# Retention attention and two expert layers in one kernel: attention reordered chunk by chunk over the batches

## The chip, the cores and the metric

The kernel runs on one core of a Trainium2 chip. The metric is the device time of one execution in microseconds (us). Three runs of the kernel before took 872.59, 873.83 and 874.82 us; the median is 873.83 us. Profiles are of a single execution, whose own time stands in the table below.

## The reference

Three stages follow one another. The first is a linear attention with a decaying state (4 batches, 8 heads, 768 tokens, 64 elements a head), the second a layer of 512 to 2048 to 512 with a piecewise quadratic activation, the third one of 512 to 1024 to 512 with a softmax gate and a normalisation. The weights are float64.

```python
for t in range(S):                       # attention, per batch and head
    state = gamma * state + outer(k[t], v[t])
    y[t] = scale * (q[t] @ state)
x = y.transpose(0, 2, 1, 3).reshape(3072, 512)
h = x @ w_in                             # first layer
g = where(h >= 1, h, where(h <= -1, 0, (h + 1) ** 2 / 4))
x = g @ w_out
h = x @ w_in2                            # second layer
solu = h * softmax(h)
out = (layernorm(solu) * g_ln) @ w_out2
```

## The kernel before

**Attention in chunks.** A unit u is one chunk of 128 tokens of one batch with all 8 heads (4 pairs of heads); there are 24. With `b, c = divmod(u, NCH)` (NCH = 6) the units run through a batch before the next begins. For each unit `att_scores` (L532) multiplies keys and queries on TensorE into PSUM `pa`; VectorE multiplies the scores by a decay table with the causal mask (`sm`, L557) and, for a chunk that isn't the first of its batch, the queries by another table (`qn`, L539). `att_products` adds the product with the state (`cross`) and the product of masked scores and values (`within`, L602 and L607), and forms the chunk's own contribution to the state (`state`, L616) from the keys, which were decayed before by GpSimd for the units 0 to 3 (L544) and by ScalarE for the others (L548). ScalarE decays the one state tile (L694) and VectorE adds the contribution (L704 for a first chunk, L706 else). In the units 0 to 11 the state tile holds two heads in the diagonal blocks of a 128x128 matrix and `cross` is four products of the full array (mode "words", L591); from unit 12 (`QUAD`) on it holds 64x64 blocks and `cross` is eight products of 64 rows by 64 columns (mode "quarters", L587). For that the second half of the head pairs is kept with swapped partitions: `load_swapped` fetches the queries and keys of the units 12 to 23 in three transfers each, and `swap_tables` exchanges the tables in between.

**Blocks.** Four units fill one block of 512 tokens, `x`. Blocks 0 and 1 are split into a high and a low part (L646, L650) and go through the first layer with plain products: `moe_h` (L748) and `moe_out` (L805), twelve products of 512 columns each per hidden block f. In the order `segs`, block 0 takes f = 0 to 5, block 1 f = 0 to 11, then each the rest. Blocks 2 to 5 go in two pairs through a version with seven products in place of eight (L986, L1137). The second layer follows (L1460, L1571, L1603). The units 0 to 3 run before the first `moe_h`, the units 4 to 15 between the hidden blocks of the first two blocks, the units 16 to 23 between the products of the first pair.

**Weights.** `conv` turns a float64 weight block into a high and a low float32 part: a load of 512 KB (L380), three ops on ScalarE, five on VectorE (L398, L401 of 256 columns' length; L404, L407, L426 of 512). The blocks f = 0 to 5 of both matrices are the first twelve.

**The order of the work.** All tasks go to a planner (`Plan`). It takes a cost for each, works back from TensorE's sequence to a goal for every other task (`late`), and lists the tasks engine by engine, the earliest goal first among those that can start (`listed`). The order that it finds is written out for TensorE, VectorE, ScalarE, GpSimd and SP; each engine then works in that order and waits for its operands. SP issues all transfers, with at most eight under way. The value `due` in most calls isn't used for goals. TensorE's tasks may swap places within a window of six during the first part.

**The start.** The prologue issues 40 warm-up products (L1212). `tables` (L453) loads the decay table in four transfers of 128 KB (L458), multiplies it on VectorE (L460) and masks it on GpSimd (L461); the table for the queries is a transfer of 256 KB (L465) and a product on GpSimd (L466).

## Time and profile before

| | |
|---|---|
| median of three runs | 873.83 us |
| profiled execution | 875.24 us |
| its span, first to last instruction | 873.2 us |
| mean granted TensorE clock | 0.991 of full speed |
| TensorE (PE) busy | 847.3 us, 97% |
| VectorE (DVE) busy | 716.4 us, 82% |
| ScalarE (ACT) busy | 577.6 us, 66% |
| GpSimd (POOL) busy | 164.1 us, 19% |
| moved by DMA | 176.09 MB, mean 202 GB/s |

TensorE's busy time counts the modelled ends of pipelined products, so consecutive products overlap in it; the step from the start of one group to the start of the next is the better measure of what a group occupies. The share of 97% is a mean over stages. The idle time that a row gives stands ahead of its group, with the work whose end released it; "issue" means that the profile shows no such work.

### The profile page before, as it was taken

The page shows a single profiled execution, that of the slowest core. Times are in us where ns is not written, and L with a number is a line of the kernel's source. Part 1 is how long each engine was busy: PE and PEld are TensorE (multiplying, and loading weights), DVE is VectorE, ACT ScalarE, POOL GpSimd, SP SyncE. Part 2 cuts the span into 40 slices and gives each one's busy share as a digit, 9 for nine tenths or more (in the row PEclk, how much of TensorE's full clock was granted, in tenths as well). Part 3 has the DMA queues.
Part 4 walks back from the last instruction along what each step waited for, and adds up shares of the span by engine and source line. Part 5 has one row for each costly group of instructions (what it writes and reads, how often), then busy time and mean ns, then how long its engine had stood idle before and what let it go on. Part 6 is the DMA issues. An engine that isn't in the chain of part 4 may idle for free.

```text
span 873.2 us, 13826 instructions
## 1 busy us (share of the span) xinstructions
PE 847.3 (97%) x4752; PEld 690.7 (79%) x4752; DVE 716.4 (82%) x1326; ACT 577.6 (66%) x1145; POOL 164.1 (19%) x421
## 2 busy tenths in 40 slices
PE   7799999999999999999999999999999999999997
PEld 6678878777777778778878877887888888888886
DVE  3999989989956887999999768899977777777761
ACT  2888857689767998885448666444655555555552
POOL 3000000000000101100141110011374444444443
PEclk7999999999999999999999999999999999999999
DMA  8956797999779999778665555767020102020001
GB/s 318 391 196 231 254 311 269 319 332 321 241 229 345 383 290 377 252 301 283 225 220 196 192 184 189 245 240 241 8 78 19 66 25 73 26 73 24 26 25 48
DMA packets 70261, 176.09 MB, mean 202 GB/s; under 512 B 7984, under 2 KB 18608, under 8 KB 70192
## 3 DMA queue, kind: packets, MB, share of 16 engines
q1 hardware_dynamic: 70192, 175.22, 57.5%
q8 instruction: 37, 0.61, 0.3%
q14 instruction: 32, 0.26, 0.1%
HBM read 124.86 MB, written 50.33 MB: 201 GB/s over the span
## 4 chain that ended last, share of the span: by engine, by line
PE 68%; DVE 15%; ACT 9%; DMA 4%; issue 3%; SPq 1%; POOL 0%; ACTq 0%; DVEq 0%
PE op L1603 15%; PE hp L986 15%; PE h2p L1460 12%; PE yp L1137 11%; PE acc L805 4%; PE hp L748 4%; DVE go L1104 3%; PE tp L1571 2%; PE pa L532 2%; DVE g L907 2%; DMA w_raw<-in_w_out_dram 1%; DVE sm L557 1%; ACT cs L727 1%; PE pa L607 1%; DVE ws L872 1%
## 5 line engine op out<-in xcount | busy, mean ns | idle before, releaser
L1137 PE MATMUL yp<-go,left 128*128 128x512 f32 x672 | 153.9, 390 | 0.9 <-ACT cs L1160 0.7
L1137 PEld LDWEIGHTS yp<-go,left 128*128 128x128 f32 x672 | 126.0, 188 | 28.2 <-ACT cs L1160 1.6
L986 PE MATMUL hp<-xoh,left 128*128 128x512 f32 x448 | 122.4, 395 | 2.0 <-issue 1.1
L1100 ACT ACTIVATE go<-g 128x512 fp32r<-128x512 f32 x112 | 69.4, 628 | 51.6 <-PE yp L1137 28.2
L986 PEld LDWEIGHTS hp<-xoh,left 128*128 128x128 f32 x448 | 82.6, 188 | 21.4 <-issue 1.9
L1603 PE MATMUL op<-w,lh 128*128 128x512 f32 x384 | 93.2, 390 | 0.9 <-ACT lh L1578 0.9
L1460 PE MATMUL h2p<-w,x2h 128*128 128x512 f32 x336 | 92.5, 397 | 0.5 <-ACT h2p L1473 0.4
L1603 PEld LDWEIGHTS op<-w,lh 128*128 128x128 f32 x384 | 71.9, 188 | 16.3 <-ACT lh L1578 1.5
L1104 DVE TENSOR_TENSOR go<-g,go 128x512 fp32r<-128x512 f32 x112 | 77.9, 704 | 7.1 <-ACT go L1100 6.3
L805 PE MATMUL acc<-gh,w 128*128 128x512 f32 x256 | 72.5, 401 | 1.5 <-ACT acc L790 1.5
L1460 PEld LDWEIGHTS h2p<-w,x2h 128*128 128x128 f32 x336 | 61.3, 188 | 13.1 <-ACT h2p L1473 1.1
L748 PE MATMUL hp<-xh,w 128*128 128x512 f32 x256 | 69.9, 399 | 1.7 <-DVE cs L730 1.0
L986 PE MATMUL hp<-xol,left 128*128 128x512 f32 x224 | 69.1, 390 | 0.0
L1036 POOL TENSOR_TENSOR g<-gl,gh 128x512 f32<-128x512 f32 x16 | 22.5, 1404 | 243.4 <-ACT gh L1010 92.8
L1522 DVE TENSOR_REDUCE st<-h2p 128x1 f32<-128x512 f32 x24 | 16.5, 686 | 56.7 <-PE h2p L1460 56.7
L729 ACT ACTIVATE cs<-cs 128x512 f32<-128x512 f32 x96 | 59.3, 625 | 1.2
L748 PEld LDWEIGHTS hp<-xh,w 128*128 128x128 f32 x256 | 47.0, 189 | 12.9 <-DVE cs L730 1.9
L805 PEld LDWEIGHTS acc<-gh,w 128*128 128x128 f32 x256 | 46.2, 188 | 13.7 <-ACT acc L790 2.3
L1460 PE MATMUL h2p<-w,x2l 128*128 128x512 f32 x168 | 51.9, 390 | 0.0
L1578 ACT ACTIVATE lh<-tp 128x512 fp32r<-128x512 f32 x48 | 28.4, 596 | 33.3 <-PE tp L1571 20.4
L986 PEld LDWEIGHTS hp<-xol,left 128*128 128x128 f32 x224 | 42.1, 188 | 9.1
L1530 ACT ACTIVATE e<-h2p,st 128x512 f32<-128x512 f32 x24 | 16.5, 689 | 48.0 <-DVE st L1525 48.0
(130 smaller groups left out, 1757.0 us busy)
## 6 DMA issues: line engine op xcount, KB each, us to landing
left<-left SPq DMA_DIRECT2D x112, 512.0 KB, 4.6
left<-wsh SPq DMA_DIRECT2D x64, 256.0 KB, 4.7
kv<-in_kv_t_dram SPq DMA_DIRECT2D x24, 512.0 KB, 7.0
w_raw<-in_w_in_dram SPq DMA_DIRECT2D x24, 512.0 KB, 7.6
w_raw<-in_w_out_dram SPq DMA_DIRECT2D x24, 512.0 KB, 7.5
left<-w SPq DMA_DIRECT2D x48, 256.0 KB, 3.1
qk<-in_qk_t_dram SPq DMA_DIRECT2D x12, 512.0 KB, 6.4
x2r<-x2d SPq DMA_DIRECT2D x12, 512.0 KB, 5.3
```

Of the source, the lines that this page charges most:

```text
L532: pe.matmul(e["qp"][o][:, p, :], e["qk"][r, 1, p, :], e["qk"][r, 0, p, :], start=True, stop=True)
L729: q = ACT(A512, lambda: sc.activation(c["t"], c["t"], AF.Square), (r,), due + 0.5)
L748: pe.matmul(c["h"], cut(w, part, k), r[:, k, :], start=(n == 0), stop=(n == 3 * KD - 1))
L805: pe.matmul(acc[d], cut(w, l, d), r, start=(first and fresh and n == 0), stop=(last and n == 2), skip_group_check=True)
L986: pe.matmul(e[bank], w[i][:, k * 128:(k + 1) * 128], x[j][:, k], start=(first and m == 0), stop=(last and m == 3 * KH - 1), skip_group_che ...
L1036: h = POOL(1.1, lambda: gp.tensor_tensor(out=g(1, 1), in0=cell["s3"], in1=cell["s5"], op=ALU.add), (x, e["s5"][1], e["c11"]), v + 4)
L1100: sc.activation(t[:, 0], quarters_g(n)[q], AF.Copy)
L1104: ve.tensor_tensor(out=lo, in0=quarters_g(n)[q], in1=fl(hi), op=ALU.subtract)
L1137: pe.matmul(e["banks"][j], w[:, s, j * 128:(j + 1) * 128], g[t], start=(n == 0 and c == 0), stop=(n == NP - 1 and c == 2))
L1460: pe.matmul(bank[b], x[t][:, AT[key], k], w2i[key, k]["w"][:, part], start=(start and m == 0), stop=(stop and m == 3 * KH - 1), skip_group ...
L1578: sc.activation(c["h"][:, 4 * n:4 * n + 4], c["tp"][:, n].rearrange("a (j c) -> a j c", j=4), AF.Copy)
L1603: pe.matmul(o["p"], c[l][:, f_], w2o[f_]["w"][:, part], start=(k == 0 and f_ == 0), stop=(k == 2 and f_ == NF2 - 1))
```

## The change

The units are numbered chunk first: `c, b = divmod(u, CPB)`, so each block holds one chunk of all four batches, and the first block holds the first chunks, which have no state to read. Each batch has its own state tile of 64x64 blocks. All cross products are quarters; the swapped loads, the swapped tables and the cleared state are gone. The head order inside `x` is changed to match what the quarters write, and the rows of `w_in` are put into that order by loading each block in two transfers of 64 partitions. Rows of the output are written where the token order needs them. In the first block the values are loaded ahead of the keys in separate halves, and the state products of its four units, with a ScalarE copy into the state tiles, are issued behind the first two hidden blocks' `moe_h`. The decay table is read as one row of 4 KB and spread over the partitions by two products with a column of ones. The scores of unit 3 use other PSUM banks, and `xh` of unit 3 is made in halves. The scores of unit 1 come before the products of unit 0. In the planner, a TensorE task that follows another TensorE task is ready when the engine is free, not a fixed tail later. Some small constants of the second layer move into a pool opened after attention. Bookkeeping of the accumulator banks (`acc["banks"]`) is left out here, as is unchanged context.

```diff
             for u in after.get(t, ()):
                 todo[u] -= 1
-                u.base = max(u.base, t.start if t is u.gate or t in u.forced else t.end)
+                u.base = max(u.base, t.start if t is u.gate or t in u.forced else free["PE"] if t.eng == u.eng == "PE" else t.end)
...
-    st = attp.tile([128, NPAIR, 128], F32, tag="state", name="state", bufs=1)
+    states = [attp.tile([128, NPAIR, D], F32, tag=f"state{b}", name="state", bufs=1) for b in range(B)]
...
-    def load_swapped(dst, src):
-        n = NPAIR // 2
-        ax = (slice(None),) * (len(dst.shape) - 3)
-        nc.sync.dma_start(dst[(slice(None), *ax, slice(0, n))], src[(slice(None), *ax, slice(0, n))])
-        for h in range(2):
-            nc.sync.dma_start(dst[(slice(64 * h, 64 * h + 64), *ax, slice(n, 2 * n))],
-                              src[(slice(64 - 64 * h, 128 - 64 * h), *ax, slice(n, 2 * n))])
...
-            nc.sync.dma_start(raw.rearrange("p a t -> p (a t)"), src.bitcast(U32))
+            if heads:
+                d, s_ = raw.rearrange("p (r c) t -> p r (c t)", r=2), src.bitcast(U32).rearrange("(r i) c -> i r c", r=2)
+                for g in range(2):
+                    nc.sync.dma_start(d[64 * g:64 * g + 64], s_[:, :, 512 * g:512 * g + 512])
+            else:
+                nc.sync.dma_start(raw.rearrange("p a t -> p (a t)"), src.bitcast(U32))
...
+        l = DMA(512, load, (), due - 9, (raw_s,), run=2 if heads else 4, ahead=ahead or CAHEAD, issues=2 if heads else 1)
...
+        row = DMA(4, lambda: nc.sync.dma_start(rows, xtab_d[0:128:64].rearrange("(a r) p c -> a r (p c)", a=1)), (), -56.0)
         for o in range(2):
-            ds = [DMA(128, partial(lambda o, d: nc.sync.dma_start(dmat[64 * d:64 * d + 64, o], xtab_d[64 * o:64 * o + 64]), o, d), (), -56.0)
-                  for d in range(2)]
-            m = DVE(U512, partial(lambda o: ve.tensor_tensor(out=dmat[:, o], in0=dmat[:, o], in1=vdec[:, o::2].to_broadcast([128, NPAIR, C]), op=ALU.mult), o), ds + [a], -56.0)
+            def spread(o):
+                c[o] = ps_h.tile([128, 512], F32, tag="h", name="spread")
+                pe.matmul(c[o], ones, rows[:, o], start=True, stop=True)
+
+            def mult(o):
+                ve.tensor_tensor(out=dmat[:, o], in0=c[o].rearrange("a (p c) -> a p c", p=NPAIR), in1=vdec[:, o::2].to_broadcast([128, NPAIR, C]), op=ALU.mult)
+            s_ = Slot("h")
+            w = plan.pe(0.9, partial(spread, o), (row,), (s_,), mode="words")
+            m = DVE(U512, partial(mult, o), [w, a])
+            s_.used(m)
...
-    def swap_tables(due):
...
-        x = DMA(256, lambda: load_swapped(qdec, xtab_d), tab["read_qdec"], due, issues=3)
-        y = DMA(2, lambda: load_swapped(gdec2, gdec_d), (), due, issues=3)
-        tab["qdec"] = [POOL(1.05, lambda: gp.tensor_tensor(out=qdec, in0=qdec, in1=gdec2.to_broadcast([128, NPAIR, C]), op=ALU.mult), (x, y), due)]
...
-        b, c = divmod(u, NCH)
+        c, b = divmod(u, CPB)
...
-            if u < QUAD:
-                nc.sync.dma_start(e["qk"], qk_t[b, c])
+            nc.sync.dma_start(e["qk"], qk_t[b, c])
...
+                nc.sync.dma_start(e["kv"], kv_t[b, c])
             else:
-                load_swapped(e["qk"], qk_t[b, c])
...
+        e["lq"] = DMA(512, f, (), due, (e["qk_slot"],), run=4, ahead=12.0)
+        if c:
+            e["lv"] = e["lk"] = DMA(512, partial(g, None), (), due, (e["kv_slot"],), run=4, ahead=12.0)
+        else:
+            e["lv"] = DMA(256, partial(g, 1), (), due, (e["kv_slot"],))
+            e["lk"] = DMA(256, partial(g, 0), (e["lv"],), due)
...
-        pool = "acc" if u in (1, 2) else "h" if blk >= 2 * NOLD and u % 2 else "pa"
+        c = blk = u // CPB
+        pool = "acc" if u in (1, 2) else "h" if u == 3 or blk >= 2 * NOLD and u % 2 else "pa"
...
+            pv = views()
+            for j in range(2):
+                for r, g in ((0, 0), (1, 1), (0, 1), (1, 0)):
+                    pe.matmul(pv[r][64 * g:64 * g + 64, j, :], st[64 * r:64 * r + 64, 2 * g + j],
+                              e["qn"][64 * r:64 * r + 64, 2 * g + j, :], start=(j == 0), stop=False, skip_group_check=True)
+
+        def within():
+            pv = views()
+            kv, sm = e["kv"], e["sm"]
+            for r in (1, 0):
                 for j in range(2):
                     for g in range(2):
-                        for r in range(2):
-                            o = r ^ g
-                            pe.matmul(pv[r][64 * o:64 * o + 64, j, :], st[64 * r:64 * r + 64, 2 * g + j, :D],
-                                      e["qn"][64 * r:64 * r + 64, 2 * g + j, :], start=(j == 0), stop=False, skip_group_check=True)
-            else:
-                for p in range(NPAIR):
-                    pe.matmul(pv[:, p, :], st[:, p, :], e["qn"][:, p, :],
-                              start=(p == 0), stop=False, skip_group_check=True)
...
+                        p = 2 * g + j
+                        pe.matmul(pv[r][64 * g:64 * g + 64, j, :], kv[:, 1, 2 * p + r, :], sm[r][:, p, :],
+                                  start=(first and j == 0), stop=(j == 1), skip_group_check=True)
...
-            _, sp = views()
-            kv = e["kv"]
+            if first:
+                e["sp"] = ps_acc.tile([128, 512], F32, tag="acc", name="sp")[:, :256].rearrange("a (p d) -> a p d", p=NPAIR)
+            sp, kv = e["sp"], e["kv"]
             for p in range(NPAIR):
                 for r in range(2):
-                    h = 2 * p + (r ^ (p // 2 if quad else 0))
+                    h = 2 * p + r
...
         ta = tb = None
         if not first:
-            ta = plan.pe(0.4 if quad else 0.89, cross, [e["sm_task"][r] for r in range(2 if quad else 1)] + [e["qn_task"], st_task[0]], mode="quarters" if quad else "words")
...
-        for x in (t, tb):
-            if x:
-                e["kv_slot"].used(x)
+        t = plan.pe(0.82, within, [e["sm_task"][r] for r in (1, 0)] + [e["lv"], ta], mode="halves")
+        e["kv_slot"].used(t)
+        sp_slots = e["pa_slots"]
+        if not last:
+            if first:
+                sp_slots = [Slot("acc")]
+
+            def sums():
+                tb = plan.pe(0.42, state, [e["scores"], e["sm_task"][1], e["lk"], t] + e["kd"], sp_slots if first else (), mode="halves")
+                e["kv_slot"].used(tb)
+                return tb
+            if not first:
+                tb = sums()
         for r in range(2):
             e["sm_slot"][r].used(t)
...
+            both = e["pa_slots"][0].pool == "pa"
+            for n, r in enumerate((None,) if both else (1, 0)):
+                a = ACT(A512 if both else A256, partial(h, r), (t,), v + 0.2, w["slots"] if cb == 0 and not n else ())
+                done += [a, DVE(U512 if both else U256, partial(l, r), (a, t), v + 0.9)]
...
+            for n, g in enumerate((1, 0)):
+                done.append(ACT(A256, partial(f, n, g), [t, e["qn_task"]] + done[:1], v + 0.2,
                                 xw[blk]["slots"] if not n and cb == 0 and not away else ()))
             if away:
-                z = DMA(256, lambda: nc.sync.dma_start(xrd[blk][:, :, tk], e["qk"][:, 0] if first else e["qn"]), done, v + 4, run=0.5)
...
         if last:
             return
-        xs = []
-        if not first:
-            dec_by, w = (gdec2, D) if quad else (gdec, 128)
-
+        if first:
...
+                x = st_wrote[b] = ACT(A256, lambda: sc.activation(st, e["sp"], AF.Copy), (sums(),))
+                sp_slots[0].used(x)
+            e["state"] = begin_state
...
             def f(p):
...
-            dec = [ACT(A64 if quad else A128, partial(f, p), [ta] + tab["gdec"], v + 0.4) for p in range(NPAIR)]
-        if quad and first:
...
-                r = slice(64 * o, 64 * o + 64)
-                if first:
-                    xs.append(DVE(U256, partial(lambda r: ve.tensor_copy(st[r, :, r], e["sp"][r]), r), [tb] + tab["st"] + [st_task[0], st_task[1]] + xs, v + 0.6))
...
+                sc.activation(st[:, p], st[:, p], AF.Copy, scale=gdec[:, p, :])
...
-                wi[f] = conv(w_in[f], due, pair=words.get(("i", f // 2)))
+                wi[f] = conv(w_in[f], due, pair=words.get(("i", f // 2)), heads=True)
...
-    for f, u in ((att_scores, 0), (att_products, 0), (att_scores, 1), (att_scores, 2), (att_products, 1), (att_scores, 3), (att_products, 2), (att_products, 3)):
+    for f, u in ((att_scores, 0), (att_scores, 1), (att_products, 0), (att_scores, 2), (att_products, 1), (att_scores, 3), (att_products, 2), (att_products, 3)):
...
-        if s == XNEW + 7:
-            swap_tables(plan.clock)
         g = moe_h(blk, f)
+        for n in (2 * s, 2 * s + 1):
+            if n < CPB:
+                cells[n]["state"]()
...
-        idc["t"] = const.tile([128, 128], F32, tag="ident", name="ident")
+        idc["t"] = late().tile([128, 128], F32, tag="ident", name="ident", bufs=1)
         nc.sync.dma_start(idc["t"], ident_d)
-    ident_dma = DMA(64, load_ident, (), 0, run=0.5, ahead=60.0)
+    ident_dma = DMA(64, load_ident, att_end, 0, run=0.5, ahead=60.0)
...
-            c["st"] = const.tile([128, 16], F32, tag="st", name="st", bufs=6)
-            c["bn"] = const.tile([128, 2, 6], F32, tag="bn", name="bn", bufs=6)
+            c["st"] = late().tile([128, 16], F32, tag="st", name="st")
+            c["bn"] = late().tile([128, 2, 6], F32, tag="bn", name="bn")
...
-        os.used(DMA(256, lambda: nc.sync.dma_start(out[t * 128:(t + 1) * 128, :], o["o"]), (x,)))
+        row = (t % TPB * NCH + t // TPB) * 128
+        os.used(DMA(256, lambda: nc.sync.dma_start(out[row:row + 128, :], o["o"]), (x,)))
```

## Rows read from the trace of the kernel before

**Rows 1.** Stages: us from-to, length, busy (instructions) PE PEld DVE ACT POOL, PEclk, DMA share, GB/s.
```profile
0.00:30.00 30.00, 20.00 (x225) 18.16 (x225) 15.05 (x28) 10.66 (x22) 7.51 (x12) 0.83 0.91 343
30.00:80.00 50.00, 47.85 (x366) 37.05 (x367) 49.06 (x94) 44.66 (x98) 0.00 (x0) 1.00 0.75 274
8.30:18.60 10.30, 7.94 (x76) 7.34 (x78) 4.79 (x9) 0.60 (x1) 2.72 (x3) 0.50 1.01 396
300.00:400.00 100.00, 99.44 (x687) 79.90 (x684) 90.49 (x150) 88.37 (x188) 8.06 (x6) 1.00 0.87 308
```

**Rows 2.** Timeline, TensorE, 0 to 34 us: start, us, line, operation, count, idle before, releaser.
```profile
1.07 4.23 PE L1212 MATMUL wps<-wz 128*128 128x128 bf16 x40 [1.07 <-DVE wz L1209]
9.15 2.08 PE L532 MATMUL pa<-qk 64*128 64x128 f32 x16 [3.86 <-DMA qk<-in_qk_t_dram]
...
20.02 1.16 PE L532 MATMUL pa<-qk 64*128 64x128 f32 x16
...
32.24 2.11 PE L748 MATMUL hp<-xh,w 128*128 128x512 f32 x8 [0.69 <-ACT xh L646]
```

**Rows 3.** Timeline, VectorE, 57 to 60 us.
```profile
57.96 0.68 DVE L404 SCALAR_TENSOR_TENSOR wm<-w_raw,wm 128x512 uint32<-128x512 uint32 x1
58.56 0.42 DVE L401 TENSOR_SCALAR wm<-wm 128x512 uint32<-128x512 uint32 x1
58.90 0.69 DVE L407 CUSTOM_DVE_ANT_0 wm<-wm,wp 128x1024 uint16<-128x1024 uint16 x1
```

**Rows 4.** Tile w, 0 to 90 us: count, ns min/median/max, first and last start.
```profile
L426 DVE TENSOR_TENSOR w<-wm,w x12: 674/685/693, 31.1 to 79.4; 128x512 fp32r<-128x512 f32 x12
```

**Rows 5.** Timeline, SP's transfers, 0 to 40 us.
```profile
1.23 2.47 SPq L458 DMA_DIRECT2D dmat<-in_xtab_dram  x4
...
4.37 0.43 SPq L505 DMA_DIRECT2D qk<-in_qk_t_dram  x1
...
23.34 0.33 SPq L511 DMA_DIRECT2D kv<-in_kv_t_dram  x1
```

**Rows 6.** Timeline, TensorE, 117 to 203 us.
```profile
118.98 1.05 PE L591 MATMUL pa<-qn,state 128*128 128x128 f32 x8
119.79 1.62 PE L805 MATMUL acc<-gh,w 128*128 128x512 f32 x6
...
195.14 1.52 PE L748 MATMUL hp<-xh,w 128*128 128x512 f32 x6
196.50 0.62 PE L805 MATMUL acc<-gh,w 128*128 128x512 f32 x2
...
199.31 0.67 PE L587 MATMUL pa<-qn,state 64*64 64x128 f32 x16
199.91 1.65 PE L805 MATMUL acc<-gh,w 128*128 128x512 f32 x6
...
202.41 0.64 PE L616 MATMUL pa<-kv 128*64 128x64 f32 x16
202.98 0.73 PE L805 MATMUL acc<-gh,w 128*128 128x512 f32 x2
```

**Rows 7.** Groups of VectorE, 0 to 80 us: shapes, count, busy us, mean ns, idle before.
```profile
L539 DVE TENSOR_TENSOR qn<-qk,qdec 128x512 f32<-128x512 f32 x6 | 4.6, 766 | 1.0 <-PE pa L591 1.0
...
L706 DVE TENSOR_TENSOR state<-pa,state 64x256 f32<-64x256 f32 x8 | 3.4, 420 | 1.3 <-ACT wp L395 0.6 <-ACT cs L727 0.5
L704 DVE COPY state<-pa 64x256 f32<-64x256 f32 x4 | 1.7, 420 | 2.4 <-PE pa L607 2.4
```

**Rows 8.** DMA issues, 0 to 45 us: count, KB each, median us to landing.
```profile
kv<-in_kv_t_dram SPq DMA_DIRECT2D x8, 512.0 KB, 10.2
```

**Rows 9.** Timeline, TensorE, 117 to 133 us: the longest stall after the start.
```profile
127.98 2.08 PE L532 MATMUL pa<-qk 64*128 64x128 f32 x16 [2.14 <-issue]
```

**Rows 10.** Timeline, all engines, 14 to 21 us: GpSimd's products and a scaling beside them.
```profile
14.27 1.04 POOL L544 TENSOR_TENSOR kv<-kv,vdec 128x512 f32<-128x512 f32 x1 [2.77 <-DMA kv<-in_kv_t_dram]
...
19.71 2.49 POOL L544 TENSOR_TENSOR kv<-kv,vdec 128x512 f32<-128x512 f32 x2 [4.40 <-DMA kv<-in_kv_t_dram]
...
20.13 1.17 DVE L539 TENSOR_TENSOR qn<-qk,qdec 128x512 f32<-128x512 f32 x1 [1.01 <-PE pa L591]
```

More of the change, by code (lines that the diff above doesn't have):

```diff
@@ L620, in att_products @@
         if not first:
-            ta = plan.pe(0.4 if quad else 0.89, cross, [e["sm_task"][r] for r in range(2 if quad else 1)] + [e["qn_task"], st_task[0]], mode="quarters" if quad else "words")
+            ta = plan.pe(0.4, cross, [e["sm_task"][r] for r in range(2)] + [e["qn_task"], st_wrote[b]], mode="quarters")
             e["qn_slot"].used(ta)
-            st_task[1] = ta
-        def sums():
-            return plan.pe(0.42, state, [e["scores"], e["sm_task"][1], e["lk"], ta] + e["kd"], mode="halves")
-        if not last and not quad:
-            tb = sums()
-        t = plan.pe(0.82, within, [e["sm_task"][r] for r in (1, 0)] + [e["lk"], ta], mode="halves")
-        if not last and quad:
-            tb = sums()
-        for x in (t, tb):
-            if x:
-                e["kv_slot"].used(x)
+        t = plan.pe(0.82, within, [e["sm_task"][r] for r in (1, 0)] + [e["lv"], ta], mode="halves")
[8 more added lines that the diff above has]
+                return tb
+            if not first:
+                tb = sums()
         for r in range(2):
@@ L777, in moe_out @@
         if first:
-            acc["slots"] = [Slot("acc") for _ in range(KD)]
+            acc["slots"], acc["banks"] = [Slot("acc") for _ in range(KD)], {}
             if not fresh:
-                before = acc["last"]
+                before, banks = acc["last"], acc["banks"]
                 for n in range(2):
@@ L794, in moe_out @@
                     s_.used(*begun[-2:])
+        banks = acc["banks"]
         def p(part):
```

147 lines of the change are left out of this document (55 added, 92 removed).

## The prediction

> **What bounds the kernel now.** I read the stages first. From 300 to 400 us TensorE is busy 99.44 of 100 us at a granted clock of 1.00; from 30 to 80 us it is busy 47.85 of 50 and VectorE 49.06 of 50; from 0 to 30 us TensorE is busy only 20.00, VectorE 15.05, and the clock averages 0.83 [rows 1]. So whatever can be won lies in the first 30 us, in TensorE work that is taken away, or in single stalls. TensorE's own sequence of the start comes next: 40 warm-up products end at 5.30, the first scores begin at 9.15 after 3.86 us without data, and the first expert product begins at 32.24 [rows 2]. Between these lie four attention chunks of one batch. Each needs the state that the chunk before it left, so scores, mask, cross product, state sum and state write follow one another over three engines.
>
> The third view is VectorE alone. Its ops follow each other every 0.60 us at 512 columns and every 0.34 us at 256 [rows 3]. The last of the twelve weight conversions of the first six hidden blocks begins at 79.4 us [rows 4], so VectorE, nearly without a gap since 30 us, delivers these weights only just in time: a second bound beside TensorE. Starting TensorE earlier helps only as far as VectorE gets earlier too.
>
> **The first block without state.** The four chunks become chunk 0 of the four batches. Gone ahead of the first expert product are three cross products, three of the query scalings and the six state writes of chunks 0 to 2; the four state products move behind the first two expert blocks. What sets the new start? Data: SP spends 1.23 to 3.70 on four table loads of 128 KB before it issues any attention data [rows 5]; a row of 4 KB replaces them, so the first query load should go out near 2.0 instead of 4.37. The goals in the planner put queries, V halves and the first expert weight ahead of the K halves. Four times 0.75 MiB and two weight blocks of 0.5 MiB are 4.2 MB; at the 396 GB/s of the stretch 8.3 to 18.6 [rows 1], from about 3.5 us, they are in at 14.1 us.
>
> TensorE ends its warm-up at 5.30 and then spreads the table in two products of 512 fp32 columns, which the trace of before doesn't have. Nearest is the cross product of four times 128 fp32 columns, 0.81 us (118.98 to 119.79) [rows 6]; I take 0.8 each, hidden if the first queries land after 6.9 us, with 0 and 3.2 (both at half clock) as ends. The first table multiply can then start at 6.4. From there VectorE has to do, until the first expert product, two table multiplies, eight masks, four splits and one weight conversion (three ops of 512 columns, two of 256): 14 times 0.60 plus 2.48 = 10.9 us. Without a gap it ends at 17.3. How many gaps? Before, 14.95 us of the first 30 are idle [rows 1]; about 9.8 of them precede the first mask, which follows the scores that end at 11.23 [rows 2], and some 5.1 follow. With the state chain gone I keep 4 of these: start at 21.5. Ends: 17.5 (no gap) and 25. The latter is half clock: the first scores took 2.08 us at a clock of 0.50 against 1.16 at full [rows 1, 2]; if the clock falls again, four scores and four value products take some 4 us each pair, 16 us from 6.9, and then come the last eviction and split, together 1.3. So the first term is 32.24 - 21.5 = **10.7 us earlier**.
>
> **What TensorE gets back.** Four state products now lie behind the start, 0.57 us each by start to start (202.41 to 202.98) [rows 6]: +2.3. Of the units 4 to 23 before, seven do their cross product in words (0.81) and become quarters (0.60, 199.31 to 199.91) [rows 6]: -1.5. Units 6, 12 and 18 were first chunks without a cross product and get one: +1.8. State products there stay sixteen. Together +2.6, so TensorE's side of the sum is -10.7 + 2.6 = **-8.1 us**. The Trainium skill, TensorEngine Tiling (Array Packing), section Overview, counts a 64x64 layout as four independent tiles, up to four times as fast where both dimensions are small. By that the eight quarter products pass half the columns of the four word products, an estimate of 0.41 us, and the seven would give 1.3 us more; the row shows 0.60, with what the change of layout costs in it, and the sum uses the row.
>
> **Whether VectorE can follow.** Up to 80 us it was busy 15.05 + 49.06 = 64.1 and idle 15.9 [rows 1]. Twelve state writes (four L704, eight L706) become four sums, eight times 0.34 = 2.7 less; six query scalings become four, 1.2 less [rows 3, 7]. The work is 60.2. Idle: 6.3 before the first multiply, the 4 of gaps, 0.9 as before after 30 us. So the twelfth conversion ends near 71.4 instead of 80.1: -8.7. The later side decides, TensorE's: **-8.1**.
>
> **Edits at nothing.** ScalarE copies the first states (four ops of 256 columns), decays K for one more chunk (u = 5) and makes fewer evictions and no table swap; its 5.3 free us in the stretch 30 to 80 cover that [rows 1]; uncovered it delays splits by at most these ops, 2 to 3 us, and the ends for this are -1 and +3. SP issues 24 query loads fewer and 9 table loads fewer, and 16 weight loads and 4 K/V halves more; at 0.33 to 0.6 us an issue [rows 5] that is some -6 to +2 us of SP time beside landings that take 10.2 us anyway [rows 8], so nothing. The output in another row order writes the same tiles, the constants moved into a later pool are the same size, the planner's rule on TensorE following TensorE alters the order of work that TensorE does without gaps: I take 0. Single stalls remain: 2.14 us ahead of the scores at 127.98, which then took 2.08 at a lowered clock [rows 9]. A new order can lose such a stall or find another; value 0, ends -4 and +4.
>
> **Sum.** The profiled execution took 875.24 us (span 873.2 and 2.0 around it); less 8.1 it is 867.1. Its time is 1.4 above the median of three, 873.83, so on the median's scale **865.7 us**.
>
> **Rivals.**
> 1. VectorE becomes the bound. GpSimd decays the K of the four first chunks, 1.04 us each [rows 10], in a stretch where VectorE now has no free time; a scaling on VectorE that ran beside two of them took 1.17 us against its mean of 0.77 [rows 7, 10]. If each of the four products of 1.04 us held VectorE for its whole length, its side is -8.7 + 4.2 = -4.5: **869.3**. For: 99% busy from 30 us on. Against: the row lost only some 0.4. The half clock above ends in the same place (start 25, -4.6). The Trainium skill, SBUF — State Buffer, section SBUF: two separate sides, calls the port that GpSimd and VectorE share an exclusive lock: the loser waits for the whole instruction, so by it the 4.2 is the price. The trace agrees that one waits (1.17), and shows a part of a length, not a whole one.
> 2. Everything closes up. No gaps, start at 18.0: TensorE's side -14.2 + 2.6 = -11.6, and the 2.14 us stall goes: **860.1**. For: no chunk waits for another. Against: eviction, split and mask of each chunk still alternate between engines.
> 3. Slower: the deferred state products stand in TensorE's queue, and behind them all expert products. They need the K halves, last in the queue's order. If these go out only where the sixth chunk's K/V did before (23.34 [rows 5]) and land 10.2 us later [rows 8], at 33.5, four GpSimd products of 1.04 end at 37.7; TensorE wants the last near 28 (21.5, twice twelve products of 512 columns at 1.36 us for six [rows 6], two pairs of state products), so it stands 10 us, then some 1 us of scores at half clock: -8.1 + 11 = +2.9, **876.7**. It decides once K lands after about 30.7. Against: by goals K goes ahead of the third weight.
> 4. It doesn't do what it says: the first expert weight, not attention, sets the start. Then the start stays near 31 and the moved products cost: -1.2 + 2.6 = +1.4, **875.2**. Against: VectorE has room for that conversion once the scalings are gone.
>
> **How the numbers follow.** My forecast has a chance of 0.52, rival 1 0.20, rival 2 0.15, rival 3 0.07, rival 4 0.06. The forecast's own range is 862 to 869 (two or three us of gaps either way). The range for 8 in 10 leaves out the far part of rival 2, and rivals 3 and 4: 859 to 872. Faster by over 0.3% (2.6 us, about what a measurement of this kernel can tell from no change): nearly all of the forecast, rival 2 and five sixths of rival 1, 0.83. Within: the rest of rival 1 and most of rival 4, 0.09. Slower: rival 3 and a little of 4, 0.08.
>
> **What would show it.** The first expert product (a product of xh and w into hp) near 21.5, no cross product ahead of it; the clock not at 0.50 between the spread and the first expert product; the twelfth conversion near 71; the four state products at 0.57 us with no wait ahead of them; 20 groups of quarters at 0.60 us. From 300 us of before on, the trace should be the old one shifted by some 8 us. I am wrong if the first expert product comes at 21 but VectorE's twelfth conversion still ends after 76, if TensorE waits for K, or if stalls after 100 us add more than 4 us.

## The result, and the profile after

The changed kernel took 863.95 us (median of 4 runs, 863.27 to 865.68) against 873.50 (4 runs, 872.59 to 874.82): a ratio of 0.9893, interval 0.9873 to 0.9912, or 9.5 us faster. The forecast was 865.7, and its mechanism is visible: the first expert product begins at 23.01 us, 9.2 earlier, with no cross product ahead of it. But two of the forecast's terms were wrong and cancelled in part; the experiments below look for which.

The stages of the kernel after (columns as in [rows 1]; the second stage of that group is 30 to 80 us too):

```profile
0.00:30.00 30.00, 24.88 (x258) 19.89 (x259) 20.02 (x36) 12.88 (x24) 7.49 (x11) 0.94 0.94 283
30.00:80.00 50.00, 49.14 (x412) 39.10 (x411) 47.48 (x92) 45.35 (x110) 0.00 (x0) 1.00 1.01 310
300.00:400.00 100.00, 98.28 (x607) 78.48 (x606) 88.31 (x141) 70.43 (x127) 7.32 (x5) 1.00 0.80 283
```

In the first 30 us TensorE works 24.88 us instead of 20.00 and VectorE 20.02 instead of 15.05. One figure went the wrong way: the DMA engines are busy for a share of 0.94 against 0.91, yet move 283 GB/s where they moved 343 [rows 1].

TensorE's timeline after, 5 to 32 us, answering to [rows 2]:

```profile
5.11 1.98 PE L456 MATMUL spread<-rows,ones 1*128 1x512 f32 x4
7.02 2.84 PE L520 MATMUL pa<-qk 64*128 64x128 f32 x32
...
16.57 1.26 PE L578 MATMUL pa<-sm,kv 128*64 128x128 f32 x16 [1.11 <-DVE sm L545]
19.02 1.25 PE L578 MATMUL pa<-sm,kv 128*64 128x128 f32 x16 [1.20 <-DVE sm L545]
20.77 0.69 PE L588 MATMUL sp<-kv 128*64 128x64 f32 x16 [0.49 <-POOL kv L532]
22.39 0.69 PE L588 MATMUL sp<-kv 128*64 128x64 f32 x16 [0.94 <-POOL kv L532]
23.01 2.11 PE L720 MATMUL hp<-xh,w 128*128 128x512 f32 x8
...
25.96 0.69 PE L588 MATMUL sp<-kv 128*64 128x64 f32 x16
```

The spread products take 1.91 us together, TensorE waits for no transfer itself, and the waits that are left are for VectorE's masks and for GpSimd's decayed keys. TensorE had two of the four state products in its order ahead of the first expert product and waited 1.43 us there for the keys.

VectorE's last split of the first block (`xl`, it ends at 21.66), and its operations beside GpSimd's four products with the keys, which begin at 19.68, 21.30, 23.57 and 25.43:

```profile
20.14 0.86 DVE L393 TENSOR_SCALAR wm<-wm 128x512 f32<-128x512 f32 x1
20.92 0.74 DVE L633 TENSOR_TENSOR xl<-pa,xh 128x256 fp32r<-128x256 f32 x2
21.59 1.03 DVE L396 TENSOR_SCALAR wm<-wm 128x512 uint32<-128x512 uint32 x1
...
23.93 0.97 DVE L393 TENSOR_SCALAR wm<-wm 128x512 f32<-128x512 f32 x1 [0.58 <-ACT wm L386]
...
26.20 1.09 DVE L421 TENSOR_TENSOR w<-wm,w 128x512 fp32r<-128x512 f32 x1 [0.36 <-ACT w L413]
```

VectorE's last scaling for the twelfth conversion (it was at 79.4 [rows 4]), and the place of the long stall of [rows 9], after:

```profile
72.76 0.69 DVE L421 TENSOR_TENSOR w<-wm,w 128x512 fp32r<-128x512 f32 x1
```

```profile
121.05 1.07 PE L779 MATMUL acc<-gl,w 128*128 128x512 f32 x4
125.10 2.08 PE L520 MATMUL pa<-qk 64*128 64x128 f32 x16 [2.98 <-ACT xr L651]
127.10 3.78 PE L720 MATMUL hp<-xh,w 128*128 128x512 f32 x8
```

**A balance.** The span can be cut at two marks: the start of the first expert product, and the start of the first product of the first pair (L986 before, L960 after). Between them count TensorE's idle time and half of the time at the half granted clock (work goes about half as fast there: the scores take 2.08 us against 1.16 [rows 2]); the rest is work. The last column is where VectorE's last scaling for the twelfth conversion begins. One profiled execution each, in us; labels are those of the experiments, "again" is the changed kernel a second time:

| kernel | start | idle | half the low-clock time | rest | from the second mark | span | twelfth conversion |
|---|---|---|---|---|---|---|---|
| before | 32.2 | 7.3 | 1.7 | 221.4 | 610.6 | 873.2 | 79.4 |
| after | 23.0 | 7.1 | 3.4 | 220.5 | 610.0 | 864.0 | 72.8 |
| after, again (e12) | 24.2 | 4.6 | 1.7 | 220.4 | 610.7 | 861.7 | 75.2 |
| e1, state products later | 24.0 | 2.4 | 3.0 | 221.7 | 609.8 | 860.8 | 76.1 |
| e2, table by four loads | 25.4 | 4.6 | 1.5 | 221.3 | 611.3 | 864.2 | 78.8 |
| e3, w_in straight | 21.5 | 6.0 | 3.5 | 219.3 | 609.5 | 859.8 | 71.5 |
| e4, before with row table | 29.6 | 7.6 | 0.0 | 221.4 | 610.7 | 869.3 | 76.8 |
| e5, no cross products | 23.2 | 7.7 | 1.7 | 213.4 | 606.9 | 852.8 | 73.0 |
| e6, K/V whole | 28.8 | 4.9 | 0.0 | 219.8 | 609.9 | 863.4 | 77.0 |
| e7, before, no state chain | 30.1 | 10.4 | 3.5 | 220.5 | 610.4 | 874.9 | 81.2 |
| e8, more on VectorE | 24.4 | 11.1 | 3.4 | 220.7 | 612.6 | 872.3 | 87.4 |
| e9, less on VectorE | 23.9 | 1.1 | 1.7 | 221.1 | 611.3 | 859.2 | 73.2 |
| e10, clamp on GpSimd | 23.8 | 2.9 | 2.0 | 220.0 | 610.1 | 858.8 | 73.7 |
| e11, e1 and e10 together | 24.7 | 2.4 | 1.7 | 221.5 | 612.0 | 862.4 | 74.8 |

Apart from e5, which leaves work out, the rest and the last part lie within 2.4 and 3.1 us for all kernels. Where a stall falls into low clock it counts in both columns, and the rest is too small by 0.5 us in after, 0.6 in e3 and 0.4 in e8. What moves the time is the start and what stalls follow it. Two executions of the changed kernel differ by 2.3 us of span (4.1 less in stalls and low clock, 1.9 more in the start and the last part), so a single profile can't settle an effect of 2 us, nor a start that differs by 1; medians decide below. Between the profiles of before and after: start -9.2, idle -0.2, clock +1.7, rest -0.9, last part -0.6, together -9.2.

### The profile page after: what moved, and what is told of

Read it like the earlier page. It is cut to its first block, busy times and chain, and to the rows that moved or that the text cites. A ratio compares the mean times of both kernels' runs of the same rounds, so it can differ in the third digit from the quotient of the medians.

```text
span 864.0 us, 13933 instructions
## 1 busy us (share of the span) xinstructions
PE 843.9 (98%) x4836; PEld 686.3 (79%) x4836; DVE 712.4 (82%) x1316; ACT 563.8 (65%) x1124; POOL 157.2 (18%) x419
## 3 DMA queue, kind: packets, MB, share of 16 engines
q1 hardware_dynamic: 67156, 174.43, 59.2%
## 4 chain that ended last, share of the span: by engine, by line
PE 77%; DVE 9%; DMA 7%; ACT 4%; issue 1%; SPq 1%; POOL 0%; ACTq 0%; DVEq 0%
PE hp L960 17%; PE op L1587 15%; PE h2p L1444 12%; PE yp L1111 11%; PE hp L720 7%; PE acc L779 6%; DMA w_raw<-in_w_out_dram 3%; DVE go L1078 3%; PE tp L1555 2%; PE pa L520 2%; PE pa L578 2%; DMA left<-wsh 2%; DVE g L881 1%; PE pa L568 1%; DMA kv<-in_kv_t_dram 1%
## 5 line engine op out<-in xcount | busy, mean ns | idle before, releaser
L960 PE MATMUL hp<-xoh,left 128*128 128x512 f32 x448 | 122.3, 395 | 1.3 <-DVE g L702 1.0
L960 PEld LDWEIGHTS hp<-xoh,left 128*128 128x128 f32 x448 | 82.5, 188 | 21.1 <-DVE g L702 1.9
L779 PE MATMUL acc<-gh,w 128*128 128x512 f32 x256 | 69.6, 400 | 0.5 <-ACT cs L793 0.5
L960 PE MATMUL hp<-xol,left 128*128 128x512 f32 x224 | 69.1, 390 | 0.0
L720 PE MATMUL hp<-xh,w 128*128 128x512 f32 x256 | 66.2, 402 | 1.4 <-DVE cs L702 1.4
L960 PEld LDWEIGHTS hp<-xol,left 128*128 128x128 f32 x224 | 42.0, 188 | 9.0
L699 ACT ACTIVATE cs<-g,half 128x512 f32<-128x512 f32 x48 | 34.3, 721 | 20.6 <-DVE g L1004 10.8
```

The source lines that it names most:

```text
L699: sc.activation(c["t"], get_h(), AF.Relu, bias=half, scale=0.5)
L720: pe.matmul(c["h"], cut(w, part, k), r[:, k, :], start=(n == 0), stop=(n == 3 * KD - 1))
L779: pe.matmul(banks[d], cut(w, l, d), r, start=(first and fresh and n == 0), stop=(last and n == 2), skip_group_check=True)
L960: pe.matmul(e[bank], w[i][:, k * 128:(k + 1) * 128], x[j][:, k], start=(first and m == 0), stop=(last and m == 3 * KH - 1), skip_group_che ...
```

## The experiments

The planner draws up the order of work anew for each edit. In e12, the same kernel, TensorE's order of groups is the same, and in e4 it is that of the kernel before but for the spread. In all others it leaves that of the edited kernel within the first 23 groups. So a difference of one or two us can come from the new order and not from what the edit names. Where medians of different comparisons stand side by side (e1, e2, e4 and e6 are one comparison, e5, e7, e8 and e9 another, e3 and e10 to e12 the third), the ratios to before are the safer measure.

**e1_states_later.** The four first state products go behind the expert blocks 2 and 3 of the order.

```diff
-        for n in (2 * s, 2 * s + 1):
-            if n < CPB:
+        for n in (2 * s - 2, 2 * s - 1):
+            if 0 <= n < CPB:
```

> The changed kernel with the four first state products one hidden block later (behind the second and third block instead of the first and second). Theory A (TensorE's queue sets the start: in the changed kernel the first expert product at 23.0 stands behind two state products that wait for the K halves): the first expert product comes at 21.7, right behind the last split (VectorE's xl ends at 21.66); the two products that moved cost 2 x 0.61 behind it, so the end stays within 1 us, 863 to 865. Rival B (the split or the weight sets the start, the state products only fill its wait): the start stays at 22.5 to 23.2 and the time grows by 1.2, 865. Rival C (VectorE's conversions govern the rest): start 21.7, twelfth conversion still at 72.8, time as before or worse.

862.52 us, ratio to before 0.9874 [0.9855, 0.9893]. The state products no longer stand ahead of the first expert product, and yet it didn't come earlier (24.0): another wait took their place.

```profile
18.53 1.09 PE L578 MATMUL pa<-sm,kv 128*64 128x128 f32 x16 [3.43 <-DMA kv<-in_kv_t_dram]
...
23.96 3.75 PE L720 MATMUL hp<-xh,w 128*128 128x512 f32 x8 [2.01 <-DVE xl L633]
```

The last V half landed late in this execution. The wait for keys was thus not a cause by itself: data came late for whichever product was next. The time is that of the changed kernel within the intervals.

**e2_table_loads.** The changed kernel with the decay table read by four loads again, without the spread.

```diff
-                pe.matmul(c[o], ones, rows[:, o], start=True, stop=True)
...
+            ds = [DMA(128, partial(lambda o, d: nc.sync.dma_start(dmat[64 * d:64 * d + 64, o], xtab_d[64 * o:64 * o + 64]), o, d), (), -56.0)
+                  for d in range(2)]
```

> The changed kernel with the decay table read again by four transfers of 128 KB, no spread product. Theory A (issue time of the table loads counts in full at the start): queries go out at about 4.3 instead of 2.0, TensorE idles from 5.3 to about 8.5 and its clock falls for longer; first expert product at 25 to 25.5, time +2 (866). Rival B (VectorE's work sets the start, loads are hidden): start 23.0 to 23.5, time 864 to 864.5.

866.86 us, ratio 0.9919 [0.9896, 0.9941]: by the medians 3 us slower than the changed kernel, by the ratios 2.3 to 2.9 (the intervals overlap), its start 2.4 later than in one execution of it and 1.2 later than in the other.

**e4_before_row_table.** That part alone on the kernel before (the same edit the other way).

> The kernel before with one part of the change alone: the decay table from a row of 4 KB and two spread products. Theory A (the chain through the state of one batch sets the start before): the first expert product at 30.5 to 32, time 0 to -1.5 against before (872 to 873.5). Rival B (the loads set the start in both): the start comes 2 us or more earlier still, 27 to 29, time -3 to -5.

871.37 us, ratio 0.9983 [0.9971, 0.9995]. The start is 2.6 earlier, the median 1.9; the time lies between what the two theories gave. The two runs agree: the row and the spread bring some 2 us of the 9.5, 3 at most by e2.

**e6_kv_whole.** Keys and values of the first four units in one load each.

```diff
-            e["lv"] = DMA(256, partial(g, 1), (), due, (e["kv_slot"],))
-            e["lk"] = DMA(256, partial(g, 0), (e["lv"],), due)
+            e["lv"] = e["lk"] = DMA(512, partial(g, None), (), due, (e["kv_slot"],), run=4)
```

> The changed kernel with K and V of the first four units in one load each of 512 KB instead of V first and K later. Theory A (bytes ahead of the last value product count: 0.5 to 0.75 MB more come ahead of the last V, at 0.4 MB a us): the first expert product 1.3 to 2 us later, 24.5 to 25, less the waits of the state products for K (1.4 us), time 864 to 865.5. Rival B (VectorE's order sets the start): start 22 to 23, since the state products no longer wait for K, time 863 to 864.

865.13 us, ratio 0.9901 [0.9882, 0.992]. The start fell back to 28.8, with waits for data of 2.12, 1.54 and 1.10 us ahead of it and the clock at half from 18.4 to 28.7, and the end hardly moved: idle 4.9 and no low clock between the marks against 7.1 and 3.4. Starting 5.8 us later cost one or two. Theory A's time came out, but not by its start of 24.5 to 25. So the time isn't the start alone: here a later start met fewer stalls. Against the kernel before, this one starts only 3.4 us earlier and yet took 8.2 less (873.29 in the same comparison).

**e5_no_cross.** The changed kernel without its 20 cross products (attention then sees only its own chunk).

```diff
-                    pe.matmul(pv[r][64 * g:64 * g + 64, j, :], st[64 * r:64 * r + 64, 2 * g + j],
-                              e["qn"][64 * r:64 * r + 64, 2 * g + j, :], start=(j == 0), stop=False, skip_group_check=True)
...
```

> The changed kernel without the twenty cross products (the product of queries and state is left out of the sum). Theory A (from the first expert product on TensorE governs, so each group of quarters costs its 0.60 us): 20 x 0.60 = 12 us less, 852. Rival B (VectorE or single stalls govern up to 260 us, where 16 of the 20 lie): only the eight groups after 250 us pay, 4 to 6 us, 858 to 860.

854.04 us, ratio 0.9777 [0.9756, 0.9798], 9.4 to 9.9 less than the changed kernel's two medians, nearly 0.5 for each. By the balance, the twelve ahead of the second mark are worth 220.5 - 213.4 = 7.1, 0.59 each, about the step of 0.60 by which the prediction priced them; the eight behind it are worth 3.1, 0.39 each. TensorE's work pays for the most part: some 10 of the 12 us that theory A gave.

**e7_before_no_chain.** The kernel before without the three cross products of the units 1 to 3, so that no chunk of the first block waits for a state (the wait of these products for the state is taken out of the plan too).

```diff
-            else:
+            elif u >= CPB:
...
```

> The kernel before without the three cross products of units 1 to 3 (the state's part of their output is left out); loads, scalings and state writes stay. Theory A (the state chain of the first batch makes most of the early idle time): the first expert product at 25 to 27 instead of 32.2, time 867 to 868.5 against 873.5. Rival B (loads, VectorE's work and the weights set it): start at 30 or later, time 871.5 to 873.

875.71 us, ratio 1.0027 [1.0017, 1.0037]: no gain, even 2 to 3 us lost. The start came 2.1 us earlier, as rival B has it, although the first queries came 1 us later; the time is above both theories. Waits stand where the chain had been:

```profile
10.14 2.08 PE L532 MATMUL pa<-qk 64*128 64x128 f32 x16 [4.62 <-DMA qk<-in_qk_t_dram]
13.73 1.12 PE L616 MATMUL pa<-kv 128*64 128x64 f32 x16 [1.51 <-issue]
...
26.68 1.01 PE L616 MATMUL pa<-kv 128*64 128x64 f32 x16 [2.87 <-issue]
...
30.09 2.50 PE L748 MATMUL hp<-xh,w 128*128 128x512 f32 x5 [0.69 <-ACT xh L646]
```

By the balance, 3.1 us more idle and 1.8 more low clock behind the start took the 2.1 back. That the chain of states makes the whole early idle time is not borne out: alone it is worth 2 us of the start here and nothing of the time. It may help along with the rest (the state products moved off the start, values ahead of keys, queries sooner, less on VectorE); no run shows these parts one by one.

**e8_vector_more, e9_vector_less.** The clamp of the first twelve conversions (the program plans it at the length of 256 columns; by its row it covers 128 by 512 elements, 0.42 us by itself and 0.34 from start to start) three times, and not at all (e9 then leaves very small and large weights as they are).

```diff
-        t3 = DVE(U256, v0, (t1,))
+        t3 = t1
+        for _ in range(clamps):
+            t3 = DVE(U256, v0, (t3,))
...
```

> The changed kernel with VectorE's clamp of the first twelve weight conversions done three times (24 more ops of 256-column length, 0.34 us each, 8.2 us on VectorE ahead of the twelfth conversion). Theory A (TensorE governs and VectorE has slack of a few us): less than half of it shows, +1 to +4 us, 865 to 868. Rival B (VectorE governs the first 75 us): the twelfth conversion 8 us later (81) and +7 to +8 us, 871 to 872. Rival C (VectorE has ample slack): below +1.

> The changed kernel with VectorE's clamp of the first twelve weight conversions left out (12 ops, 4.1 us less on VectorE; the clamp of tiny and huge weights is left out). Theory A (TensorE governs): the first expert product comes 0 to 0.7 us earlier (one conversion and part of a second lie ahead of it), time -0.5 to -1, 863 to 863.5. Rival B (VectorE governs the first 75 us): -3 to -4 us, 860 to 861.

With 8.2 us more, 874.94 us, ratio 1.0023 [1.0012, 1.0035], about 11 slower than the changed kernel; with 4.1 us less, 860.41, ratio 0.986 [0.9848, 0.9873], 3.5 faster by the medians and 2.3 to 2.9 by the ratios. TensorE in e8 from its start to 80 us, then in e9 in three stretches (columns as above):

```profile
24.40:80.00 55.60, 46.28 (x411) 36.39 (x409) 47.93 (x94) 42.56 (x105) 3.43 (x3) 0.94 0.95 301
```

```profile
23.90:80.00 56.10, 55.86 (x473) 44.48 (x470) 52.36 (x91) 50.80 (x120) 3.81 (x4) 0.97 1.04 317
80.00:100.00 20.00, 19.95 (x88) 16.23 (x87) 19.36 (x41) 18.00 (x36) 0.00 (x0) 1.00 0.78 263
100.00:247.80 147.80, 146.97 (x1029) 117.92 (x1029) 142.71 (x268) 120.47 (x272) 0.00 (x0) 1.00 0.92 321
```

In e8 TensorE stands 9.3 us before 80 us. In e9 it stands 0.2 there, but the changed kernel has only 0.9 to win; the gain comes after 100 us, where idle time falls from 4.9 (4.2 in e12) to 0.8. So work added on VectorE in the first 80 us isn't absorbed: the twelfth conversion begins at 87.4 instead of 72.8 and 75.2, and more than the 8.2 us shows in the time. That less work is what won in e9 isn't shown: its twelfth conversion begins at 73.2, between the changed kernel's two, and its TensorE has another order where the long stall stood (see e10). VectorE isn't busy throughout: in e8 it stands 7.7 of these 55.6 us itself, so the loss is not VectorE's busy time alone; that two engines wait for each other in fixed orders fits this.

**e3_straight_w_in.** The changed kernel with w_in's blocks loaded in one transfer each.

```diff
-                wi[f] = conv(w_in[f], due, pair=words.get(("i", f // 2)), heads=True)
+                wi[f] = conv(w_in[f], due, pair=words.get(("i", f // 2)))
```

> The changed kernel with w_in's blocks loaded straight, in one transfer each: its rows are not put into the order of the heads (so the output is of another matrix), 16 transfers fewer on SP. The prediction priced the halves at nothing: 863 to 865.7 like the changed kernel, within 1 us. The rival: smaller pieces of 4 KB a partition cost the queue or the twelve first weights; then the twelfth conversion ends 1 to 3 us earlier and the time is 861 to 862.5.

859.35 us, ratio 0.9842 [0.9822, 0.9861]; the changed kernel in the same comparison took 863.43 (e12). So the halves cost 4.1 us, and the time is below the rival's 861 to 862.5. Its first stage, and TensorE's start:

```profile
0.00:30.00 30.00, 27.07 (x289) 22.41 (x292) 21.44 (x41) 14.91 (x32) 7.66 (x11) 0.89 0.93 357
```

```profile
18.03 1.78 PE L578 MATMUL pa<-sm,kv 128*64 128x128 f32 x16 [1.20 <-DVE sm L545]
19.60 1.93 PE L588 MATMUL sp<-kv 128*64 128x64 f32 x32
21.45 2.20 PE L720 MATMUL hp<-xh,w 128*128 128x512 f32 x8
```

The transfers of the first 30 us, the changed kernel and then this one (count, KB each, median us to landing):

```profile
w_raw<-in_w_in_dram SPq DMA_DIRECT2D x10, 256.0 KB, 9.5
kv<-in_kv_t_dram SPq DMA_DIRECT2D x8, 256.0 KB, 8.9
```

```profile
w_raw<-in_w_in_dram SPq DMA_DIRECT2D x6, 512.0 KB, 8.1
kv<-in_kv_t_dram SPq DMA_DIRECT2D x8, 256.0 KB, 7.9
```

And SP behind the second weight block, the changed kernel and then this one:

```profile
7.25 1.35 SPq L373 DMA_DIRECT2D w_raw<-in_w_in_dram  x2
9.45 2.49 SPq L496 DMA_DIRECT2D kv<-in_kv_t_dram  x3
```

```profile
5.91 0.45 SPq L375 DMA_DIRECT2D w_raw<-in_w_in_dram  x1
6.98 2.44 SPq L496 DMA_DIRECT2D kv<-in_kv_t_dram  x3
```

SP's order of loads is the same in both. Two halves took SP 1.35 us where a whole block took 0.45, and the loads behind them went out 2.5 us later. At an equal busy share the DMA engines move 357 GB/s instead of 283. The reordered block travels as 256 pieces of 2 KB, the straight one as 128 of 4 KB. By the trace's packet records of these 30 us, a piece of 2 KB took 115 ns on average with the reordered loads against 87 without, and one of 4 KB 197 against 166: the other transfers got slower too. The size of the pieces, the half of the partitions and the second issue were changed together; no run tells them apart. The keys' products begin 3.0 us earlier (GpSimd's first at 16.71 against 19.68), and TensorE waits for none. By the balance the start accounts for 1.5 to 2.8 of the 4.1 us; where the rest arises isn't shown. All this holds although a stall of 5.66 us ahead of 118.38 and the low clock that begins in it happen to stand in this execution. The Trainium skill, DMA: Bandwidth & Descriptors, section Rules for kernel authors, advises against two transfers to disjoint partition halves, since both use the same engines; the trace agrees (283 against 357 GB/s), and shows a price beyond the second issue.

**e10_clamp_gpsimd, e11_clamp_and_later, e12_after_again.** The clamp of eight of the first twelve conversions on GpSimd; the same with e1's order; and the changed kernel for the comparison.

```diff
-        t3 = DVE(U256, v0, (t1,))
+        t3 = POOL(0.7, v0, (t1,)) if side else DVE(U256, v0, (t1,))
...
```

> The changed kernel, with one of the VectorE operations (the clamp, 0.34 us) of eight of the first twelve weight conversions given to GpSimd, which otherwise only decays K there. Theory A (VectorE's own time in the first 80 us sets the order and the stalls behind it, as when twelve clamps were left out and 3.5 us were won): 8 x 0.34 = 2.7 us of VectorE less, so 1.5 to 3 us faster than the changed kernel, ratio to it near 0.997. Theory B (VectorE waits out the length of each GpSimd operation beside it): eight times about 0.7 to 1 us of waiting replace 2.7 us of work, so 3 to 5 us slower than the changed kernel, and VectorE's operations beside the clamps are lengthened by that much.

> The same, with the four first state products behind blocks 2 and 3 (the order that came out near 862.5 before). Theory A: both add up, 859.5 to 861.5. Theory B: 865 to 868. A third possibility: the order after 80 us is drawn anew by each of them and the sum is between 860 and 865 whatever VectorE saves; then the stall near 125 us shows whether it is in this order.

> The changed kernel itself, run with the others for the comparison: 863 to 865.7, first expert product at 23.0, a stall of about 3 us near 125 us.

e12: 863.43 us, ratio 0.9886 [0.9867, 0.9904]; the stall stands in it with 1.92 us. e10: **859.61 us**, ratio 0.9844 [0.9821, 0.9866], 3.8 under e12 and the fastest kernel that leaves nothing out; it has no stall near 125 us (idle between the marks 2.9 against 4.6). Theory B fell. Theory A has the sign, but the gain is more than its 1.5 to 3, and the order may explain part of it: the scores that waited 2.98 us in the changed kernel behind the `acc` products stand ahead of these in e10.

```profile
120.03 1.16 PE L520 MATMUL pa<-qk 64*128 64x128 f32 x16
121.13 2.11 PE L779 MATMUL acc<-gh,w 128*128 128x512 f32 x8
```

They do so in e1, e9 and e11 too, and the stall near 125 us is gone in all four; in e12 and e6 they stand behind, and it is there. In e1 VectorE was relieved of nothing. So how much of the 3.8 us is VectorE's relief and how much the new order stays open. GpSimd's work in e10's first 80 us, and three VectorE groups in 30 to 72 us, first of e10, then of e12:

```profile
L393 POOL TENSOR_SCALAR wm<-wm 128x512 f32<-128x512 f32 x8 | 16.2, 2029 | 19.4 <-ACT wm L386 17.2 <-DVE w L421 2.2
```

```profile
L421 DVE TENSOR_TENSOR w<-wm,w 128x512 fp32r<-128x512 f32 x9 | 6.5, 724 | 0.7 <-ACT w L413 0.7
...
L396 DVE TENSOR_SCALAR wm<-wm 128x512 uint32<-128x512 uint32 x9 | 5.4, 598 | 0.7 <-POOL wm L393 0.7
...
L527 DVE TENSOR_TENSOR qn<-qk,qdec 128x512 f32<-128x512 f32 x4 | 3.1, 782 | 0.0
```

```profile
L421 DVE TENSOR_TENSOR w<-wm,w 128x512 fp32r<-128x512 f32 x9 | 6.2, 686 | 0.2
...
L396 DVE TENSOR_SCALAR wm<-wm 128x512 uint32<-128x512 uint32 x9 | 3.8, 418 | 0.0
L527 DVE TENSOR_TENSOR qn<-qk,qdec 128x512 f32<-128x512 f32 x4 | 2.7, 682 | 0.0
```

Beside 16.2 us of GpSimd, these three groups lost 0.3 + 1.6 + 0.4 = 2.3 us. It comes once per clamp: beside six of the eight, one VectorE operation took 0.39 to 0.42 us longer than elsewhere, and the next ones took their usual time although the clamp went on. Beside the clamp from 41.89 to 43.93:

```profile
42.07 1.10 DVE L527 TENSOR_TENSOR qn<-qk,qdec 128x512 f32<-128x512 f32 x1
43.09 0.68 DVE L399 SCALAR_TENSOR_TENSOR wm<-w_raw,wm 128x512 uint32<-128x512 uint32 x1
```

The Trainium skill, SBUF — State Buffer, section SBUF: two separate sides, has the loser of the shared port wait for a whole instruction; here VectorE paid about a seventh of GpSimd's time. e11, 863.83, ratio 0.9889 [0.9869, 0.9909], didn't add up: the third possibility. Its stalls up to the second mark are gone (idle 2.4), but two more state products lie behind the start, and 1.3 us more than in e12 fall behind the second mark, where a wait of 2.0 us for `g` stands.

## Why the prediction was right, and where its steps were not

**Start: 21.5 forecast, 23.0 (and 24.2) measured.** Inside its ends. VectorE's last split of the block ended at 21.66 (21.01 in e12), where the forecast put the start. Behind it TensorE still had two of the state products in its order, which the prediction had placed behind the start, and waited for their keys. These came late with all early data, and there the prediction missed one of its "edits at nothing": the halves of w_in were priced as SP's time alone, 16 issues more, and at nothing. They cost 4.1 us of the time (e3), and with them all early transfers were slower. "In at 14.1 us" rested on 396 GB/s; from 2 to 16 us it was 292, and 352 with straight loads. With these the start is 21.45 and the twelfth conversion ends at 72.1, near the forecast (21.5 and 71.4), though two state products stand ahead of the start there too and the last split ended at 20.70. This is the mis-sized term of the sum.

**Why the chain alone was not the reason.** The prediction gave the gaps to the chain of states. e7 shows that without it, in the kernel before, the start comes 2.1 us earlier and nothing is won in the time. What the first term holds is the sum of its parts; only the row table (some 2 us, e2 and e4) has been sized alone. And the start is not the whole gain: e6 has 3.4 of its 9.2 us and 8.2 of the 9.5 us of time.

**What TensorE gets back: +2.6 forecast, -1.5 measured** (rest -0.9, last part -0.6; together -1.1 if the low clock inside the stall counts once). Two of the four state products were ordered ahead of the start, so only 1.1 of 2.3 came back behind it. The step of a quarter cross, 0.60, held up (0.59 in e5). That leaves about 3 us. The traces place most of it between the marks: by steps from start to start, with low clock taken out, the 256 products of `xh` took 61.0 us before and 59.2 after (59.0 in e12), in 32 unbroken groups instead of 58, and the products of scores and values 11.7 and 11.1. The prediction took the new order of TensorE's work at 0. Whether the planner's new rule makes that order is not shown: no run takes the rule away alone. The rest and the last part each scatter by about one us between kernels with the same work there (221.4 and 220.5 in before and e7).

**VectorE: -8.7 forecast, -6.7 measured** (72.76 against 79.43), and only -4.3 in e12 (75.16). The 4 us of gaps came out in the first execution: from the first multiply to 30 us VectorE stands 4.0 us, but 7.5 in e12. Its work up to the end of this conversion was 62.0 us instead of 60.2 (60.3 in e12). Rival 1's cause is part of that: beside GpSimd's four products, one VectorE operation each was longer than elsewhere, by 0.44 + 0.61 + 0.55 + 0.41 = 2.0 us (1.1 in e12), half of the 4.2 that the rival charged. But the step "the later side decides" is not borne out. In e12 VectorE's side stood about where rival 1 put it (-4.5), and the time was 863.43 and not 869.3; in e1 the conversion began at 76.1, and the time was 862.52. What e8 shows is that VectorE has no room for more work there.

**Stalls: 0 forecast.** The stall of 2.14 us at 127.98 [rows 9] became one of 2.98 at 125.10, and in e12 of 1.92; it is gone in e1, e9, e10 and e11. Between the marks idle and low clock together cost 1.5 us more than before in one execution and 2.7 us less in the other: within the ends of 4.

**The other rivals.** Everything closing up (860.1) is near what straight loads and e10 bring, 859.4 and 859.6: it was 4 us away, not excluded, though no start came near its 18.0. Waiting for K was real but 1.43 us (2.0 in e12), not 11, because the halves landed before 25.4 us, where the last of GpSimd's products begins. Rival 4 fell with the start at 23.0.

**The signs that it named.** No cross product stands ahead of the first expert product, the groups of quarters step by 0.60 us, and the later stretch is the old one shifted by 8.7 us at the second mark and 9.3 at the end: these came out. The clock stood at 0.50 for 3.4 us from 8.1, between the spread and the first expert product, the state products step by 0.61 to 0.62, and TensorE waited for K, which the prediction had called a sign of being wrong: these did not.

So the total was right within 2 us by luck in the sizes: a start that came 1.5 to 2.7 us late met a return that came out some 4 us smaller.

## What to carry to other kernels

Price a transfer cut in pieces by the rate of the whole stretch, not by its issue alone: at the start, where all wait for data, loads in two half-partition transfers of 2 KB pieces took a fifth of the bandwidth. Take one suspected cause away alone before believing it: here neither the chain of states nor the wait for keys was worth anything in the time by itself. Where a planner draws up the order anew, look at the order before giving a gain to the edit: the stall near 125 us is gone in four runs of different edits, all with the scores ahead of the `acc` products. Work can be moved to an idle engine though it takes five times as long there: with 2.7 us of VectorE's work on GpSimd the kernel was 3.8 us faster, and not slower by the length of the GpSimd operations.

## What the runs showed of the hardware

A clamp of 128 by 512 floats took 2.03 us on GpSimd against 0.42 on VectorE, and slowed VectorE by 0.39 to 0.42 us beside six of eight such clamps, not by its length. GpSimd's products of 1.04 to 1.30 us cost VectorE 0.41 to 0.61 us each in the first execution. The low clock came at other places in each kernel: after, 3.4 us from 8.1 (before, 10.2 from 8.3) and 6.8 from 124.1, beginning inside the stall of 2.98 us; in the second execution 3.4 from 7.2, 6.8 from 20.8 and none near its stall of 1.92.
